# One third of a projection moved ahead of a transpose, copied twin columns and a ninth warm matmul in the first five microseconds of a fused attention and MLP kernel

## The chip, the cores and the metric

The kernel runs on one core of one Trainium2 chip. The metric is the device time of one execution in microseconds (us), lower being better. The engines are called PE (matrix multiply), ACT (activation functions and copies), DVE (vector operations), POOL and SP (which issues most DMA). A kernel is one program with a fixed instruction order on each engine; the engines wait for each other by semaphores. All runs below are of one core, mean granted clock 1.00.

## The reference

The input x is 2048 tokens by 448 features. It is normalized per token, then used twice: by linear attention with 16 heads of 28 features, and by an MLP whose hidden layer has 1792 features. The result is `x + attention * silu(mlp)`.

```python
xn  = (x - mean(x)) / sqrt(var(x) + 1e-5)            # per token
qkv = xn @ wqkv                                      # 448 -> 3 * 448, 16 heads of 28
phi = lambda t: where(t > 0, t + 1, exp(t)) + 1e-6
# attention: kv = sum_s phi(k) v ; z = sum_s phi(k) ; o = phi(q) kv / (phi(q) z + 1e-6) ; s = o @ wo
h   = relu(xn @ w1 + b1) ** 2                        # 448 -> 1792
out = x + s * silu(h @ w2 + b2)
```

All inputs are bf16. Everything starts with the normalization of x and its transposition, because the kernel's matmuls sum over the 448 features and take them on the partitions.

## The kernel before

The kernel treats the first four tiles of 128 tokens (tiles 0 to 3) by hand. For each tile, DVE takes statistics, ACT forms the reciprocal deviation, DVE writes the normalized tile `xn`, PE transposes it in chunks of 128 columns, and ACT or DVE copies the transposed chunks from PSUM to `xT`. Because 448 is three chunks of 128 and one of 64, the last 64 columns are stored twice (the "twin" columns), so that chunk 3 is a full 128 columns and its two halves can serve two matmuls of 64 rows side by side.

```python
def ln_norm(si, part=None):      # normalized columns of tile si; tiles 0 and 1 in two parts
    c = (slice(0, D if si > 3 else 384), slice(0, 256), slice(256, 384))[0 if part is None else part + 1]
    ...  # dve tensor_scalar: xn[:, si, c] = (x_tok[:, si, c] - mean) * rstd

def ln_twin(lo, hi, eng="dve"):  # tiles 4 and up: copy columns 384..448 to 448..512
    ...  # tensor_copy(xn[:, lo:hi, 448:512], xn[:, lo:hi, 384:448])

def ln_last(si):                 # tiles 0 to 3: columns 384..448 formed twice, from x itself
    ...  # dve tensor_scalar over a view of x that repeats the 64 columns; writes xn[:, si, 384:512]

def pe_transpose(si, part, eng): # part 0: chunks 0 and 1; part 1: chunks 2 and 3; None: all four
    b = Buf("T")                 # one PSUM bank
    ...  # one PE transpose per chunk
    if (si, part) == (0, 0):     # tile 0, part 0 is copied chunk by chunk
        head["xT00a"] = add(eng, lambda e, x: ev(e, x, 0, 1), [b], [("xT", 0, "a")], 0.25)
        return add(eng, lambda e, x: ev(e, x, 1, 1), [b], names, 0.25)
    return add(eng, ev, [b], names, ...)

# the PE order of the head ("turn" transposes and copies a part of a tile)
warm(8, wide=True)                                        # 8 matmuls of 512 columns on constants
turn(0, 0, "act")                                         # T00
turn(0, 1, "act")                                         # T01
turn(1, 0, "act")                                         # T10
mains(k0, (0,), [("xT", 0, "a")] + wnames("wk")[:1])      # K0, first third
mains(k0, (1,), [("xT", 0, 0)])
mains(k0, (2,), [("xT", 0, 1)])
turn(1, 1, "act")                                         # T11
mains(k1, (0, 1), [("xT", 1, 0)] + wnames("wk")[:1])      # K1, needs xT10
h_mains(0, (0, 1))                                        # first MLP tile, needs w1
...
head["xT2"] = pe_transpose(2, None, "act")                # T2
h_mains(3)
head["xT3"] = pe_transpose(3, None, "dve")                # T3
```

K0 and K1 are the key and value part of wk's product for tiles 0 and 1, each in three matmuls of 512 columns (one per chunk of 128 features). The PE order is the program order above; a matmul that waits holds up all that follow.

## Time and profile before

| | before |
|---|---|
| median of 3 runs | 141.24 us (141.20 to 141.33) |
| span of the profiled execution | 139.7 us |
| PE busy | 136.6 us, 98% |
| first matmul of K0 / of K1 | 4.92 us / 5.68 us |

The page of the kernel before: busy time with its share of the span and the number of instructions, then the chain that ended last, by engine.

```profile
PE 136.6 (98%) x1255; PEld 68.0 (49%) x1255; DVE 92.2 (66%) x226; ACT 77.8 (56%) x152; POOL 25.0 (18%) x33
...
PE 95%; DVE 2%; DMA 2%; issue 0%; DVEq 0%
```

PE is the bottleneck. What happens before PE has a continuous stream is what a change of the head can move. The timeline of the same kernel, PE only; columns are the start, the time covered, engine, line, operation, what it writes and reads, and how many instructions were merged.

```profile
2.41 1.49 PE L1062 MATMUL pb<-ones 128*128 128x512 bf16 x3
4.09 1.00 PE L528 MATMUL pb<-ident,xn 128*128 128x128 bf16 x6 [0.19 <-DVE xn L486]
4.92 0.81 PE L641 MATMUL pb<-w_qkv,xT 128*128 128x512 bf16 x3
5.57 0.28 PE L528 MATMUL pb<-ident,xn 128*128 128x128 bf16 x2
5.68 0.59 PE L641 MATMUL pb<-w_qkv,xT 128*128 128x512 bf16 x2
```

The first line is the end of the warm matmuls. Line 528 is the transposes: four of tile 0 and two of tile 1, spread out from 4.09 on. Line 641 is K0 at 4.92 (three matmuls in 0.81 us: two spacings of 0.216 and one record of 0.38), then T11, then K1 at 5.68. From 4.92 the starts follow each other without a hole.

Two more lines, from the timelines of DVE and of ACT: when tile 0's statistics start (released by the DMA of x), and when ACT copies T10.

```profile
2.22 0.63 DVE L463 BATCH_NORM_STATS2 st<-x_tok 128x6 f32<-128x448 bf16 x1 [2.02 <-DMA x_tok<-in_A_x_dram]
```

```profile
5.14 0.38 ACT L538 ACTIVATE xT<-pb 128x256 bf16<-128x256 bf16 x1
```

### The profile page before, as it was taken

What the parts mean: (1) busy time and instruction counts of PE and PEld (TensorE: products, weight loads), DVE (VectorE), ACT (ScalarE), POOL (GpSimd) and SP (SyncE); (2) the same over time, 40 slices, a digit from 0 to 9 for tenths busy, and PEclk for the clock granted to TensorE, in tenths of its full rate; (3) what the DMA queues carried; (4) which work ended last, traced back from release to release, by engine and by line L of the source; (5) the groups of instructions that cost most, each with busy time, mean ns of one, the idle gap of its engine ahead of it and who ended that gap; (6) DMA issues with size and microseconds to landing.
All of it is one profiled execution on the core that took longest, in us unless ns stands there. A gap on an engine that the chain in (4) does not pass through costs nothing.

```text
span 139.7 us, 3106 instructions
## 1 busy us (share of the span) xinstructions
PE 136.6 (98%) x1255; PEld 68.0 (49%) x1255; DVE 92.2 (66%) x226; ACT 77.8 (56%) x152; POOL 25.0 (18%) x33
## 2 busy tenths in 40 slices
PE   9999999999999999999999999999999999999992
PEld 2474444444444444444455455645555555555481
DVE  3989899799878994889995900329636071542653
ACT  4769787879988878979788912422033030301220
POOL 6000000000000000000893000000002328091770
DMA  6997367999723200000000148960000103111122
GB/s 190 247 335 219 77 170 186 356 276 144 131 52 70 60 6 0 0 19 5 0 0 0 42 120 169 175 107 0 0 0 5 66 0 101 35 66 66 38 99 68
DMA packets 20354, 12.91 MB, mean 92 GB/s; under 512 B 9524, under 2 KB 19956, under 8 KB 20340
## 3 DMA queue, kind: packets, MB, share of 16 engines
q1 hardware_dynamic: 18332, 11.52, 33.3%
q10 hardware_dynamic: 2008, 1.20, 4.3%
q8 instruction: 10, 0.16, 0.5%
q14 instruction: 4, 0.03, 0.1%
HBM read 8.78 MB, written 2.10 MB: 78 GB/s over the span
## 4 chain that ended last, share of the span: by engine, by line
PE 95%; DVE 2%; DMA 2%; issue 0%; DVEq 0%
PE pb L955 31%; PE pb L688 30%; PE pb L641 9%; PE pb L1021 8%; PE pb L722 7%; PE pb L672 6%; DMA x_tok<-in_A_x_dram 2%; PE pb L528 1%; PE pb L728 1%; DVE st L463 1%; PE pb L815 1%; PE pb L776 1%; PE pb L853 0%; DVE xn L991 0%; DVE mv L464 0%; PE pb L846 0%
## 5 line engine op out<-in xcount | busy, mean ns | idle before, releaser
L688 PE MATMUL pb<-xT,w 64*128 64x512 bf16 (+2 forms) x408 | 51.6, 365 | 0.0
L955 PE MATMUL pb<-w,r 64*128 64x448 bf16 (+3 forms) x406 | 44.9, 343 | 0.0
L697 ACT ACTIVATE r<-pb,b1f 128x512 bf16<-128x512 f32 x56 | 35.1, 688 | 4.2 <-PE pb L688 4.2
L688 PEld LDWEIGHTS pb<-xT,w 64*128 64x128 bf16 (+1 forms) x408 | 22.8, 94 | 22.5 <-ACT r L697 0.5
L955 PEld LDWEIGHTS pb<-w,r 64*128 64x128 bf16 (+1 forms) x406 | 22.8, 95 | 19.9 <-issue 0.7
L966 DVE TENSOR_TENSOR gbuf<-pb,b2b 128x448 bf16<-128x448 f32 (+1 forms) x16 | 9.2, 608 | 30.0 <-PE pb L955 30.0
L931 ACT ACTIVATE gbuf<-gbuf 128x448 bf16<-128x448 bf16 (+1 forms) x16 | 8.7, 565 | 36.0 <-DVE gbuf L966 35.5
L1000 POOL TENSOR_TENSOR xn<-xn,x_tok 128x448 bf16<-128x448 bf16 x15 | 15.0, 1032 | 46.3 <-DVE xn L991 46.3
L641 PE MATMUL pb<-w_qkv,xT 64*128 64x512 bf16 (+1 forms) x106 | 17.8, 376 | 0.0
L672 PE MATMUL pb<-xT,w_qkv 64*128 64x512 bf16 x84 | 15.5, 376 | 0.0
L705 DVE TENSOR_TENSOR r<-r 128x512 bf16<-128x512 bf16 x42 | 14.4, 418 | 0.0
L390 POOL MEMSET kvm<- 128x2048 bf16 x1 | 1.8, 1804 | 63.4 <-DVE zb L666 63.4
L1021 PE MATMUL pb<-msb,pqT 64*128 64x448 bf16 (+3 forms) x93 | 10.9, 343 | 0.0
L629 DVE SCALAR_TENSOR_TENSOR qk<-pb,qk 128x512 bf16<-128x512 f32 x16 | 10.6, 685 | 0.2
L463 DVE BATCH_NORM_STATS2 st<-x_tok 128x6 f32<-128x448 bf16 x16 | 9.3, 610 | 2.0 <-DMA x_tok<-in_A_x_dram 2.0
L991 DVE TENSOR_TENSOR xn<-pb,gbuf 128x448 bf16<-128x448 f32 (+2 forms) x17 | 9.2, 591 | 2.0 <-ACT gbuf L931 1.5
L619 ACT ACTIVATE qk<-pb 128x512 bf16<-128x512 f32 x16 | 8.9, 593 | 3.0 <-PE pb L641 2.5
L641 PEld LDWEIGHTS pb<-w_qkv,xT 64*128 64x128 bf16 (+1 forms) x106 | 6.7, 94 | 6.0 <-ACT xT L538 0.2
L722 PE MATMUL pb<-qk,xn 128*128 128x448 bf16 x48 | 9.3, 353 | 0.0
L619 ACT ACTIVATE pqT<-pb 128x512 bf16<-128x512 f32 x12 | 6.8, 597 | 3.2 <-PE pb L688 1.6
L672 PEld LDWEIGHTS pb<-xT,w_qkv 64*128 64x128 bf16 x84 | 6.0, 94 | 5.0
L706 ACT ACTIVATE r<-r 128x512 bf16<-128x512 bf16 x14 | 8.4, 637 | 0.0
(71 smaller groups left out, 99.7 us busy)
## 6 DMA issues: line engine op xcount, KB each, us to landing
out_dram<-xn SPq DMA_DIRECT2D x15, 112.0 KB, 1.7
w<-in_B_w_dram SPq DMA_DIRECT2D x1, 1568.0 KB, 10.0
x_tok<-in_A_x_dram SPq DMA_DIRECT2D x3, 448.0 KB, 3.8
xT<-rows ACTq DMA_DIRECT2D x6, 112.0 KB
w<-in_B_w_dram SPq DMA_DIRECT2D x1, 576.0 KB, 4.6
xT<-rows SPq DMA_DIRECT2D x5, 112.0 KB
w_o<-in_A_wo_dram SPq DMA_DIRECT2D x1, 392.0 KB, 11.3
w_qkv<-in_A_wqkv_dram SPq DMA_DIRECT2D x1, 384.0 KB, 3.6
```

The source lines that it names most:

```text
L463: add("dve", lambda e, _: e.bn_stats(st6[:, si, :], x_tok[:, si, :]), [("x", si)], [("st", si)], 0.58),
L619: add("act", lambda e, _: e.activation(out=slot, in_=src(), func=AF.Exp), [buf, "actw"], [tile], 0.6)
L629: lambda e, _: e.scalar_tensor_tensor(out=slot, in0=src(), scalar=1.0 + 1e-6, in1=slot, op0=ALU.add, op1=ALU.max),
L641: return e.matmul(ps(b)[:, 0:512], xT[half[h], c, si * P : (si + 1) * P], w_qkv[half[h], c, 384 : 2 * D], start=start, stop=stop,)
L672: return e.matmul(ps(b)[:, 0:512], w_qkv[half[h], c, m * P : (m + 1) * P], xT[half[h], c, g * 512 : (g + 1) * 512], start=start, stop=stop,)
L688: return e.matmul(ps(b)[:, c0 : c0 + n], w_1[half[h], c, fi * P : (fi + 1) * P], xT[half[h], c, t : t + n], start=start, stop=stop,)
L697: lambda e, _: e.activation(out=slot, in_=ps(b)[:, 0:512], func=AF.Relu, bias=b1f[:, fi : fi + 1]),
L705: return e.tensor_tensor(out=slot, in0=slot, in1=slot, op=ALU.mult)
L722: last = e.matmul(ps(b)[:, 0:D], xn[:, si, c * P : (c + 1) * P], pk_of(si), start=(si == 0), stop=(si == NT - 1),)
L955: return e.matmul(ps(b)[:, 0:n], r2[half[h], fi, si * P : (si + 1) * P], w_2[half[h], fi, c], start=start, stop=stop)
L1000: eng, lambda e, _: e.tensor_tensor(out=ob, in0=ob, in1=x_tok[:, si, c], op=ALU.add),
L1021: return e.matmul(ps(b)[:, 0:n], q, m, start=start, stop=stop)
```

## The change

There are three parts. (1) K0's first third is put ahead of T10, so that PE has a matmul to do while DVE still works on tile 1. (2) Tiles 1 to 3 get all 448 columns in one pass and copy the twins, where they had formed them from x; only tile 0 keeps the old form. (3) A ninth warm matmul fills PE's hole between the warm matmuls and T00. The scheduled order on ACT, POOL and SP is the same in both kernels; only these PE and DVE instructions differ.

```diff
-            c = (slice(0, D if si > 3 else 384), slice(0, 256), slice(256, 384))[0 if part is None else part + 1]
+            c = (slice(0, D), slice(0, 256), slice(256, D if si else 384))[0 if part is None else part + 1]
...
-            twin = head[f"xd{i}"] = ln_last(i)
+            twin = head[f"xd{i}"] = ln_twin(i, i + 1, "dve") if i else ln_last(i)
...
-        warm(8, wide=True)
+        warm(9, wide=True)
...
+        mains(k0, (0,), [("xT", 0, "a")] + wnames("wk")[:1])
         turn(1, 0, "act")
-        mains(k0, (0,), [("xT", 0, "a")] + wnames("wk")[:1])
...
-            ("dve", "st0 mv0 ... st3 mv3 xd2 xn2 xd3 xn3 xT3"),
+            ("dve", "st0 mv0 ... st3 mv3 xn2 xd2 xn3 xd3 xT3"),
```

## The prediction

> **What bounds the kernel.** TensorE. The page has PE busy 136.6 of 139.7 us, and the chain that ended last is PE for 95%. From 4.92 us the matmul records start back to back (0.216 us for 512 columns), with two small holes before 9 us: 0.10 us at 8.16 (a weight load waiting for a DMA) and 0.14 us at 8.70 (waiting for the copy xT of tile 3, which itself follows the PE). So only the first 5 us can change, and what the PE gains or loses there shifts everything after it.
>
> **The head before (timeline, records of PE, ACT, DVE).** Warm matmuls start every 0.427 us; the eighth, at 3.27, streams until 3.69. The PE then idles to 4.09, where T00 (tile 0, chunks 0 and 1) starts, released by DVE xn. Chunks 2 and 3 follow at 4.31 and 4.53, each behind its DVE producer. T10 (tile 1) follows at 4.80 and 4.87, again behind DVE xn (end 4.74). K0's first third starts at 4.92. Its input, the ACT copy xT00a, ended at 4.79, so it could have started at about 4.84.
>
> **What the change does.**
> 1. K0's first third no longer stands behind T10. It gains at most 4.92 - 4.84 = 0.08 us of start.
> 2. T10 now waits out a 0.216 us matmul: its pair runs at about 5.09 and 5.15, not 4.80 and 4.87. The ACT copy xT10 moves with it: transpose 0.22, handover 0.04, copy 0.38, handover 0.05.
> 3. The ninth warm matmul runs from 3.69 to 4.12. T00 was ready at 4.09, so T00 and xT00a come 0.03 us later, and K0's first third starts at about 4.875. The clock goes up near 4.8 (records of 0.29 us at 4.53, 0.23 at 4.80, 0.22 after). The Trainium skill, "TensorE: Matmul & The Clock Gate", Part 1, says that a busy window of about 3.4 us releases it and that the window is free-running; the hole of 0.4 us did not prevent the release here, so filling it should change little (30%: it comes earlier).
> 4. DVE: tile 1's xn11 grows from 128 to 192 columns (0.31 us, about 0.33 after), and the twin forms (0.31 us each) become copies (about 0.17, estimated from 0.20 for two tiles) that wait for their producer. st2 moves under 0.03 us; T2 and T3 get their last inputs before the PE reaches them. Worth nothing.
>
> **On the critical path.** K1's first third needs xT10. Before, that ended at 5.52 and K1 followed in PE order at 5.68. After: T10 ends at 5.37, xT10 at 5.78, K1 starts at about 5.84, though the PE reaches it at 5.75. Later work is in PE order, so the loss of 0.16 us stays; only the DMA hole at 8.16 closes, which the hole at 8.70 gives back. If the clock rises before 4.1 us instead, the loss shrinks to about 0.04.
>
> **Prediction.** 141.37 us, 8 in 10 between 141.15 and 141.55. Faster by over 2%: 0.005; within 2%: 0.99; slower by over 2%: 0.005.
>
> **What would show it.** Step 1: K0's first third at 4.84 to 4.90. Step 2: xT10 starting at 5.40 instead of 5.14, and a new PE hole of 0.09 us behind ACT xT just before K1. Step 3: T00 at 4.12, and the first 0.22 us record at the same time as before. Step 4: DVE busy down some 0.2 us.
>
> **What would make it wrong.** An earlier clock release; x landing at another time; ACT's copies overlapping more than I read, so that K1 does not wait; a window phase that differs in the timed runs by more than 0.16 us.

## The result, and the profile after

| | before | after |
|---|---|---|
| median, runs of the same rounds | 141.30 us (141.20 to 141.58, 6 runs) | 141.57 us (141.25 to 141.78, 6 runs) |
| ratio of the runs | | 1.0015, 95% interval 0.9999 to 1.0031 |
| span of the profiled execution | 139.7 us | 140.3 us |
| first matmul of K0 / of K1 | 4.92 / 5.68 us | 5.05 / 6.29 us |

A ratio is the mean time of one kernel's runs over that of the other's of the same rounds, so it is not quite the ratio of the medians. The page of the changed kernel, busy time and chain:

```profile
PE 137.3 (98%) x1256; PEld 68.5 (49%) x1256; DVE 92.1 (66%) x226; ACT 77.9 (56%) x152; POOL 25.0 (18%) x33
...
PE 98%; DVE 0%; issue 0%; DVEq 0%
```

PE is busier by 0.7 us, with one warm matmul more and some records that are longer. The Trainium skill, "Trainium Kernel Development and Optimization", Performance Expectations, warns that matmul busy time is a bad metric for how close a kernel is to roofline, because matmuls are pipelined. Busy time misleads here too, if for another reason: the useful work is the same, and reads as 0.7 us more because of the warm matmul and the cold records. The timeline of the changed kernel, PE, against the lines of before:

```profile
2.41 1.91 PE L1062 MATMUL pb<-ones 128*128 128x512 bf16 x4
4.29 0.73 PE L528 MATMUL pb<-ident,xn 128*128 128x128 bf16 x4
5.05 0.61 PE L641 MATMUL pb<-w_qkv,xT 128*128 128x512 bf16 x1
5.45 0.36 PE L528 MATMUL pb<-ident,xn 128*128 128x128 bf16 x2
5.65 0.59 PE L641 MATMUL pb<-w_qkv,xT 128*128 128x512 bf16 x2
6.08 0.27 PE L528 MATMUL pb<-ident,xn 128*128 128x128 bf16 x2
6.29 0.60 PE L641 MATMUL pb<-w_qkv,xT 128*128 128x512 bf16 x2
```

And tile 0's statistics and the ACT copy of T10 (views as before):

```profile
2.43 0.63 DVE L463 BATCH_NORM_STATS2 st<-x_tok 128x6 f32<-128x448 bf16 x1 [2.23 <-DMA x_tok<-in_A_x_dram]
```

```profile
5.85 0.38 ACT L538 ACTIVATE xT<-pb 128x256 bf16<-128x256 bf16 x1 [0.41 <-PE pb L528]
```

K1 starts 0.61 us later than before. Three things are mixed in this number:

- x landed later: statistics at 2.43 instead of 2.22, so 0.21 us. DVE's first instruction of x is ahead of everything that was changed.
- K0's first matmul took 0.61 us for its record, where the same matmul took 0.38 before, and the next start came 0.40 us after it, not 0.22. PE ran at half speed: in this execution the clock rose only near 5.6 us, in the one before near 4.8.
- The order: T10 stood behind that matmul, its copy started at 5.85, and K1 waited for it. T11's second transpose starts at 6.137 in the trace, K1 would follow 0.056 later at 6.193, and it starts at 6.289: a hole of 0.096 us.

To separate these, I use one length in every trace from here on: from the start of T00 to the start of K1's first third, called **T00 to K1**. It takes out when x lands: T00 came 1.86 us after the start of tile 0's statistics in the unchanged kernel and in the changed one. It was 1.595 before (5.681 - 4.086) and 2.001 after (6.289 - 4.288).

### The profile page after: what moved, and what is told of

It reads as the page before. It is cut to its first block, busy times and chain, and to the rows that moved or that the text cites. A ratio compares the mean times of both kernels' runs of the same rounds, so it can differ in the third digit from the quotient of the medians.

```text
span 140.3 us, 3108 instructions
## 1 busy us (share of the span) xinstructions
PE 137.3 (98%) x1256; PEld 68.5 (49%) x1256; DVE 92.1 (66%) x226; ACT 77.9 (56%) x152; POOL 25.0 (18%) x33
## 4 chain that ended last, share of the span: by engine, by line
PE 98%; DVE 0%; issue 0%; DVEq 0%
PE pb L955 30%; PE pb L688 30%; PE pb L641 9%; PE pb L1021 8%; PE pb L722 7%; PE pb L672 6%; PE pb L1062 3%; PE pb L728 1%; PE pb L528 1%; PE pb L815 1%; PE pb L776 1%; PE pb L853 0%; DVE xn L991 0%; PE pb L846 0%; DVE xn L1000 0%
## 5 line engine op out<-in xcount | busy, mean ns | idle before, releaser
L641 PE MATMUL pb<-w_qkv,xT 64*128 64x512 bf16 (+1 forms) x106 | 18.3, 379 | 0.0
```

The lines of the kernel that those rows point to most:

```text
L641: return e.matmul(ps(b)[:, 0:512], xT[half[h], c, si * P : (si + 1) * P], w_qkv[half[h], c, 384 : 2 * D], start=start, stop=stop,)
```

## The experiments

Twelve runs were made, two of them of unaltered kernels. Every run was numerically correct. All but the four delayed ones are within 0.3% of the kernel before, so the times decide little, and the traces decide.

### The parts one by one

`e1_order` (the swap alone), `e2_nine` (the ninth warm matmul alone), `e3_twins` (the twins alone), and `e4_nine_twins` (everything but the swap), against before in five rounds on one chip.

```diff
 # e1: only the swap                              # e2: only
+        mains(k0, (0,), ...)                     -        warm(8, wide=True)
         turn(1, 0, "act")                        +        warm(9, wide=True)
-        mains(k0, (0,), ...)
 # e3: only ln_norm, ln_twin and the DVE order    # e4: e2 and e3 together
```

> Only the order is changed (K0's first third ahead of T10; eight warm matmuls, old twins). Landmark: from the start of T00 to the start of K1's first third; it was 1.60 us before and 2.00 us after the whole change, which takes out when x lands. Theory A (order and clock together): the late T10 makes K1 wait for the ACT copy xT10, a hole of about 0.09 us before K1; landmark 1.72 to 1.76 if the clock rises before K0's first third, 1.95 to 2.05 if it rises after it; time 0.10 to 0.25 us over before. Rival B (the ninth warm matmul or the twins cost it): landmark about 1.60, no hole, time within 0.08 us of before. Rival C (the clock alone, which varies from run to run): no hole, the landmark goes with the time of the rise only.

> Only the ninth warm matmul is added. Theory A: T00 starts when its DVE input is there or at 4.12 us, whichever is later: at most 0.04 us, landmark 1.60 if the clock rises at about 4.8; time within 0.08 us of before. Rival B: it is the ninth matmul that moves the rise of the clock (4.81 us before, 5.60 after the change): rise near 5.6 again, time 0.2 us over before. If filling the hole helps the clock as intended, the rise comes at 4.4 or earlier.

> Only the twins of tiles 1 to 3 become copies. Theory A: DVE does as much by the time the PE asks; T2 starts in PE order with no DVE wait (the 0.01 us one before it goes), landmark 1.60, time within 0.08 us of before. Rival B: the copies that wait for their producer delay st2 or T11, time 0.1 us or more over before.

> The changed kernel with the order alone undone. Theory A: no hole before K1, time within 0.08 us of before and 0.1 to 0.25 us under the changed kernel. Rival B: as slow as the changed kernel.

| | median us (range, runs) | ratio to before (95%) | T00 to K1 |
|---|---|---|---|
| before, same rounds | 141.41 (141.21 to 143.19, 11) | 1 | |
| e1_order | 141.44 (141.31 to 141.55, 5) | 0.9991 (0.9944 to 1.0037) | 1.632 |
| e2_nine | 141.60 (141.54 to 141.84, 5) | 1.0008 (0.9966 to 1.0050) | 1.593 |
| e3_twins | 141.58 (141.19 to 141.94, 6) | 1.0000 (0.9960 to 1.0040) | 1.598 |
| e4_nine_twins | 141.45 (141.26 to 141.59, 5) | 0.9994 (0.9952 to 1.0035) | 1.979 |

No time can be told from another. (The run of 143.19 us is among those of before; without it the four ratios would be 1.0001, 1.0016, 1.0009 and 1.0002.) The lengths can, and they overthrew part of what I expected. `e4`, which has the old order, is almost as slow to K1 as the changed kernel; `e1`, which has the new order, is quick. The timeline of e4, PE:

```profile
4.20 1.11 PE L528 MATMUL pb<-ident,xn 128*128 128x128 bf16 x6
5.10 1.13 PE L641 MATMUL pb<-w_qkv,xT 128*128 128x512 bf16 x3
...
6.18 0.59 PE L641 MATMUL pb<-w_qkv,xT 128*128 128x512 bf16 x2
```

K0's three matmuls fill 1.13 us, not 0.81 as before: the first two started cold (records of 0.634 and 0.487 us). The timeline of e1, PE:

```profile
4.20 0.68 PE L528 MATMUL pb<-ident,xn 128*128 128x128 bf16 x4 [0.30 <-DVE xn L486]
4.86 0.39 PE L641 MATMUL pb<-w_qkv,xT 128*128 128x512 bf16 x1
...
5.63 0.28 PE L528 MATMUL pb<-ident,xn 128*128 128x128 bf16 x2
5.83 0.60 PE L641 MATMUL pb<-w_qkv,xT 128*128 128x512 bf16 x2
```

Here the clock was already up at T00 (records of 0.23 us, not 0.29). The swap does what it promises: K0 starts 0.66 us after T00, against 0.84 before (and 0.84 in e3, which has the old order and an early clock). But T11's second transpose is at 5.682, so K1 could have started at 5.738 and starts at 5.834, the same hole of 0.096. T00 to K1 is 1.632, against 1.595 before and 1.598 in e3, so the swap costs 0.03 to 0.04 us with an early clock. I had written 1.72 as the least in the expectation, for a clock that rises between T00 and K0; I had forgotten there the still earlier clock for which the prediction itself had said 0.04. And the expected 0.10 to 0.25 us in the time of e1 did not show either.

The trace of `e2` gives the ninth matmul nothing to answer for (its times are another matter, see below): T00 to K1 is 1.593, the clock rises near 4.65 us, neither at 4.4 or earlier, as the intent would have it, nor near 5.6, as the rival would. It showed one thing by chance. In that execution the x of tiles 2 and 3 landed late, at 5.37 us instead of 4.73, and T3 waited 0.15 us for DVE. The timeline of e2, DVE's last step for tile 3, PE's weight load and the first transposes of T3:

```profile
7.79 0.37 DVE L486 TENSOR_SCALAR xn<-x_tok,mv,rstd 128x384 bf16<-128x384 bf16 x1
...
8.22 0.23 PEld L528 LDWEIGHTS pb<-ident,xn 128*128 128x128 bf16 x4 [0.27 <-DVE xn L486]
```

With the old twins, xn of tile 3 is the last thing DVE makes; in the kernel before it ended at 7.87, and PE asked for it at 7.94. `e3` makes it ahead of its twin: there it ended 3.585 us after T00, against 3.779 before, and T3 followed in PE order at 3.835. So the twins' part makes tile 3 robust against a late x, by 0.19 us, and no more: in e3 itself nothing waited for it. The DVE timeline of before, tiles 2 and 3 (twin, norm, twin, norm), and of the changed kernel (norm, copy, norm, copy):

```profile
6.71 0.31 DVE L512 TENSOR_SCALAR xn<-x_tok,mv,rstd 128x128 bf16<-128x128 bf16 x1
6.94 0.37 DVE L486 TENSOR_SCALAR xn<-x_tok,mv,rstd 128x384 bf16<-128x384 bf16 x1
7.26 0.31 DVE L512 TENSOR_SCALAR xn<-x_tok,mv,rstd 128x128 bf16<-128x128 bf16 x1
7.49 0.37 DVE L486 TENSOR_SCALAR xn<-x_tok,mv,rstd 128x384 bf16<-128x384 bf16 x1
```

```profile
7.23 0.40 DVE L486 TENSOR_SCALAR xn<-x_tok,mv,rstd 128x448 bf16<-128x448 bf16 x1 [0.36 <-ACT rstd L477]
7.66 0.18 DVE L501 COPY xn<-xn 128x64 bf16<-128x64 bf16 x1
7.75 0.39 DVE L486 TENSOR_SCALAR xn<-x_tok,mv,rstd 128x448 bf16<-128x448 bf16 x1
8.18 0.18 DVE L501 COPY xn<-xn 128x64 bf16<-128x64 bf16 x1
```

The copies are shorter (0.18 for 0.31), but each waits for its producer's end, and the old forms overlapped: in both, the four instructions take 1.13 to 1.15 us from first start to last end.

### The clock taken out

If the rise of the clock is what blurs the picture, then a kernel whose head starts after the rise must show the swap alone. Ten dummy statistics on DVE (on the constant row, to a scratch tile) hold tile 0 back by about 4 us, and 14 more warm matmuls, gated on them, keep PE at work. By then x and the weights of the head have landed too. These kernels are slower on purpose.

```diff
+        for i in range(10):
+            head[f"dl{i}"] = add("dve", lambda e, _, i=i: e.bn_stats(dly[:, i, :], junk), ["ones"], [("dly", i)], 0.6)
...
-        warm(8, wide=True)          # (9 in the changed kernel)
+        warm(8, wide=True)
+        warm(6, wide=True, after=[("dly", 5)])
+        warm(8, wide=True, after=[("dly", 9)])
...
-            ("dve", "st0 mv0 ...
+            ("dve", "dl0 ... dl9 st0 mv0 ...
```

`e5_late_old` is the kernel before with this delay, `e6_late_new` the changed kernel (with 8 first warm matmuls, so without the ninth), `e7_late_twins` the twins alone. `e8_late_two` takes the old twins and puts two thirds of K0 ahead of T10 (`turn(1, 0, "act")` behind `mains(k0, (1,), ...)`), a larger dose of the same medicine.

> The kernel before, with ten dummy statistics on DVE ahead of tile 0 (about 6 us) and more warm matmuls behind them, so that in every execution the clock is up and x and weights have landed when T00 starts. A reference for the three below, not an attempt to be fast: about 145.5 us. Theory A (the spread between runs and between kernels is the moment the clock rises and x lands): the five runs lie within 0.15 us of each other, where before spread over 0.3 us and more; landmark T00 to K1 1.59 to 1.61. Rival C (the spread comes from elsewhere): as wide as before.

> The whole change under the same delay and the same warm matmuls. Theory A: with the clock up, the order costs only the wait for xT10, about 0.04 us: landmark 1.63, K1 behind a hole of about 0.09 us, time 0.00 to 0.06 us over the late old kernel. Rival B (the change costs 0.2 us whatever the clock does): 0.15 to 0.25 us over it. If the change pays as intended: under it.

> The twins' change alone under the same delay. Theory A: xn of tile 3 comes 0.15 to 0.2 us earlier, and nothing asks for it: time within 0.05 us of the late old kernel, landmark 1.60.

> Two thirds of K0 ahead of T10 instead of one, old twins, same delay. Theory A: T10 comes 0.22 us later still, so K1 starts at 1.83 to 1.86 behind a hole of about 0.3 us, and the time is 0.22 to 0.28 us over the late old kernel. Rival (the order does not matter, the PE does the same work in any order): landmark 1.60 to 1.65, no more than 0.05 us over it.

In all four, every transpose was recorded with at most 0.23 us, so the clock was up. The timeline of the late old kernel (T00 at 8.08, then K0 and K1), of the late new kernel (T00 and K1), and of the late kernel with two thirds ahead, PE:

```profile
8.08 0.94 PE L529 MATMUL pb<-ident,xn 128*128 128x128 bf16 x6
8.86 0.81 PE L642 MATMUL pb<-w_qkv,xT 128*128 128x512 bf16 x3
...
9.62 0.59 PE L642 MATMUL pb<-w_qkv,xT 128*128 128x512 bf16 x2
```

```profile
8.09 0.62 PE L529 MATMUL pb<-ident,xn 128*128 128x128 bf16 x4
...
9.71 0.60 PE L642 MATMUL pb<-w_qkv,xT 128*128 128x512 bf16 x2
```

```profile
8.73 0.61 PE L642 MATMUL pb<-w_qkv,xT 128*128 128x512 bf16 x2
...
9.50 0.28 PE L529 MATMUL pb<-ident,xn 128*128 128x128 bf16 x2
9.92 0.61 PE L642 MATMUL pb<-w_qkv,xT 128*128 128x512 bf16 x2
```

In the last, T11 ends its stream near 9.61 and K1 starts at 9.92, when the copy of T10 is there: a hole of 0.31 us, as expected.

| | T00 to K1 | all runs, us |
|---|---|---|
| e5_late_old | 1.540 | 145.09, 145.12, 145.19, 145.22; 146.03, 146.46 |
| e7_late_twins | 1.535 | 145.09, 145.09, 145.11, 145.14, 145.27; 146.10 |
| e6_late_new | 1.619 | 145.22, 145.27; 146.01, 146.18, 146.19, 146.29 |
| e8_late_two | 1.835 | 145.44, 145.62; 146.42, 146.42, 146.62, 146.69 |

The order matters, and in the direction of the theory: one third ahead of T10 costs 0.079 us (0.084 against e7, which has the same twins; twice the 0.04 I expected), two thirds cost 0.295, the twins nothing. Part of this is the delay's own doing: T00 came 1.90 us after tile 0's statistics here, not 1.86, because the last of the added warm matmuls held it (in e5 that matmul started at 7.865 and T00 at 8.083). In the new order K1 hangs on T00, in the old one on DVE's columns of tile 1, so a held T00 makes the swap look dearer. That is a reading, not tested. Counted from the statistics, which are not held, e6 is 0.082 behind e7. The runs fall into two groups some 0.9 us apart, which I had not expected; my forecast that the runs of e5 would lie within 0.15 us holds for the lower group only. In the lower group, the means are 145.16 (old), 145.25 (new) and 145.53 (two thirds): the differences of 0.09 and 0.37 are near those of the lengths. With two runs each for the new order and two thirds, and the upper group set aside after the fact, they are a hint and no proof.

What sets the groups apart was seen in one trace. The profiled execution of e6 was of the upper group, and its PE has one hole that the late old kernel lacks, near 43 us. The timelines of e6, PE and SP's queue:

```profile
42.03 0.59 PE L642 MATMUL pb<-w_qkv,xT 64*128 64x512 bf16 x4
43.38 0.59 PE L689 MATMUL pb<-xT,w 64*128 64x512 bf16 x3 [0.76 <-ACT r L698]
```

```profile
39.53 1.27 SPq L550 DMA_TRANSPOSE xT<-xn  x1
40.84 3.22 SPq L652 DMA_TRANSPOSE pqR<-qk  x2
```

SP took 3.22 us for the two issues after that of tile 11 (2.51 in e5), the first of them alone 1.94 instead of 1.23. The trace's semaphore record has tile 11's transposition landing at 43.29 us, against 41.93 in e5, and the weight load that needs it goes 0.06 us after the landing. The view names ACT as the releaser; ACT had been done (its last update before was at 43.01), and the DMA came last. From start to start PE lost 0.92 us there, which with the 0.08 of the head makes nearly all of the 1.00 us that e6 is behind e5 from T00 to the last matmul. Why tile 11's transposition landed late stays open: SP's slow issue was of the one behind it, so it may be a consequence as well as a sign of the same cause. The upper group held 8 of the 12 runs of e6 and e8, and 3 of the 12 of e5 and e7. Whether a later K1 makes it likelier is not tested; so I can't say that it has nothing to do with the order.

### The same kernels again, the missing combination, and a candidate

`e9_after_again` and `e10_before_again` are the two kernels unaltered. `e12_order_twins` is the changed kernel with eight warm matmuls. `e11_split` is e12 with chunk 0 of tile 0 transposed into a PSUM bank of its own, so that ACT's first copy need not wait for chunk 1. (A draft with both chunks in one bank, ordered for chunk 0 alone, was a race, since PE would write the bank that ACT reads.)

```diff
             b = Buf("T")
+            b0 = Buf("T0") if (si, part) == (0, 0) else b     # chunk 0's bank
...
-                head["xT00a"] = add(eng, lambda e, x: ev(e, x, 0, 1), [b], [("xT", 0, "a")], 0.25)
+                head["xT00a"] = add(eng, lambda e, x: ev(e, x, 0, 1), [b0], [("xT", 0, "a")], 0.25)
```

> The changed kernel once more, unaltered, for another sample of when the clock rises. Theory A (the rise falls anywhere between 3 and 6 us, and only it separates a landmark of 1.63 from one of 2.00): T00 to K1 1.63 if the clock is up before T00, 1.74 to 1.78 if it rises within 0.8 us of T00, 1.95 to 2.05 if later. Rival B (nine warm matmuls and the new order make it rise late): rise near 5.6 and landmark near 2.00 again. Time 141.3 to 141.8.

> The kernel before once more, unaltered. Theory A: landmark 1.60 if the clock is up within 0.8 us of T00, up to 1.98 if it rises later; time 141.2 to 141.8, and its runs overlap those of the changed kernel. Rival B: landmark 1.60 and 0.15 us or more under the changed kernel in each run.

> The changed kernel with eight warm matmuls. Theory A: as the changed kernel at the same moment of the rise (1.63, 1.74 to 1.78, 1.95 to 2.05), with a hole before K1 in each case. If the ninth matmul matters: another landmark at the same rise.

> The new order and twins with eight warm matmuls, and chunk 0 of tile 0 transposed into a bank of its own, so that ACT copies it without waiting for chunk 1. Theory A: K0's first third then starts about 0.08 us earlier, T10 and K1 with it: landmark 1.53 to 1.58 with an early clock (1.63 without the split), 0.05 us under the kernel before at best, which the times will not tell from it. Rival (K0's start is not what T10 waits for): 1.63.

The timeline of the unchanged kernel, second sample, PE:

```profile
4.14 1.11 PE L528 MATMUL pb<-ident,xn 128*128 128x128 bf16 x6 [0.24 <-DVE xn L486]
5.05 1.17 PE L641 MATMUL pb<-w_qkv,xT 128*128 128x512 bf16 x3
...
6.17 0.59 PE L641 MATMUL pb<-w_qkv,xT 128*128 128x512 bf16 x2
```

The timeline of the changed kernel, second sample, PE:

```profile
4.21 0.67 PE L528 MATMUL pb<-ident,xn 128*128 128x128 bf16 x4
4.87 0.39 PE L641 MATMUL pb<-w_qkv,xT 128*128 128x512 bf16 x1
...
5.84 0.60 PE L641 MATMUL pb<-w_qkv,xT 128*128 128x512 bf16 x2
```

The roles are exchanged. This time the unchanged kernel was the slow one to K1 (2.024, above the 1.98 that I had given as the most) and the changed kernel the quick one (1.631), and what differs within each pair of equal kernels is the clock. So neither the ninth matmul nor the order makes the clock late every time; rival B as I wrote it falls. That they change how often it is late is not excluded by two traces of a kernel.

The cleanest pair for the order with an early clock is e3 and e12: both have the copied twins and eight warm matmuls, both had the clock up before T00, and they differ in the order alone. The timelines of e3 and of e12, PE, T00 and K1:

```profile
4.23 1.00 PE L528 MATMUL pb<-ident,xn 128*128 128x128 bf16 x6 [0.60 <-DVE xn L486]
...
5.83 0.59 PE L641 MATMUL pb<-w_qkv,xT 128*128 128x512 bf16 x2
```

```profile
4.15 0.68 PE L528 MATMUL pb<-ident,xn 128*128 128x128 bf16 x4 [0.36 <-DVE xn L486]
...
5.78 0.61 PE L641 MATMUL pb<-w_qkv,xT 128*128 128x512 bf16 x2
```

Now all ten undelayed traces, sorted by order and clock. The second column is the start of the first PE record that is shorter than a cold one; the last is the length from T00 to the start of the last matmul of the whole kernel.

| trace | first short record, us | T00 to K1 | T00 to the last matmul |
|---|---|---|---|
| e3_twins, old order | 2.84 | 1.598 | 132.693 |
| e2_nine, old order | 4.65 | 1.593 | 132.888 (T3 waited 0.15 for DVE) |
| before, old order | 4.80 | 1.595 | 132.708 |
| e10_before_again, old order | 5.47 | 2.024 | 133.138 |
| e4_nine_twins, old order | 5.53 | 1.979 | 133.073 |
| e12_order_twins, new order | 3.27 | 1.631 | 132.853 (PE waited 0.11 for w1) |
| e9_after_again, new order | 3.69 | 1.631 | 132.734 |
| e1_order, new order | 4.20 | 1.632 | 132.905 (PE waited 0.16 at 96.7 us) |
| after, new order | 5.56 | 2.001 | 133.104 |
| e11_split, new order | 4.16 | 1.576 | 132.680 |

Whatever K1 loses, the last matmul loses too, apart from the three waits that are noted. e10 lost 0.429 to K1 against before and 0.430 at the end; after lost 0.406 and 0.396. From K1 to the last matmul every trace takes 131.09 to 131.14 us, once the three waits are taken out. That is what a saturated PE means.

The times of this batch: e9 141.66 us (141.22 to 141.91, 6 runs), ratio to before 1.0004 (0.9962 to 1.0045); e10 141.25 (141.19 to 141.60), ratio 0.9979 (0.9935 to 1.0023); e12 141.42 (141.18 to 143.05), 1.0003; e11 141.54 (141.12 to 141.76), 0.9993. Note the second: the kernel before, measured against itself in the same rounds, came out 0.21% faster, more than the 0.15% of the first result. But most of it comes from one run of 143.24 us among those of before: without it e10 is 0.06% faster, and e9, the changed kernel, 0.15% slower, as in the first result.

The times hold a hint that I had not looked for. Of the runs of the unchanged kernel, 22 of 45 are at or under 141.35 us; of the changed kernel, 2 of 12; of the other altered ones without a delay, 6 of 23 with eight warm matmuls and 1 of 10 with nine. Of the four traces with nine, two had a late clock, of the six with eight, one. The limit of 141.35 was chosen after the fact, the kernels ran on several chips, and the time of a run does not tell when its clock rose, so this may be chance. But the rival that the change, perhaps its ninth matmul, makes a late rise more frequent stands, and no run here tests it.

The split does what the theory says: K0 starts 0.60 us after T00 instead of 0.65 (0.08 was expected), K1 at 1.576 instead of 1.631. It is the first version with the new order that is ahead of the old one to K1 (1.595), by 0.02 us, and its profiled execution, 141.12 us, is the shortest of all runs. But its median is no better than the others', so it isn't shown to beat the kernel before. In e12, the MLP's first matmul waited for w1, which landed at 6.29 us. In the other nine undelayed traces it landed between 5.40 and 6.20, so this is another draw of a landing and not the faster head: e11's K1 was earlier still (5.73) and did not wait.

## Why the prediction was right or wrong

The direction (slower by a trifle) is what the lengths show; the times only lean that way, as the interval includes 1. The median of the changed kernel's six runs, 141.57, is 0.02 us over the top of my range; the ratio times the median of before, 141.30 x 1.0015 = 141.51, is inside. The size is not confirmed: the times can't resolve it. In the profiled pair the changed kernel lost 0.41 us from T00 to K1, and most of that was luck, the clock of that one execution: the pair e9 and e10 came out the other way round.

**Step 1, K0 starts earlier: right.** Seen from T00, K0 started at 0.764 instead of 0.835 with the clock still cold (after), and at 0.655 instead of 0.839 with the clock up (e1 and e9 against e3). Predicted was 4.875 - 4.12 = 0.755.

**Step 2, T10 and K1 late: the mechanism was right, the size depends on the clock.** The hole before K1 was predicted at 0.09 and measured at 0.096 in after. What it costs in T00 to K1 is 0.033 with the clock up before T00 (1.631 in e12 against 1.598 in e3, which differ in the order alone; the prediction's other case said 0.04), and 0.08 in the late kernels (e6 against e5 and e7), where T00 was held. The 0.16 of the main case, a clock that rises between T00 and K0, was never met with the new order in a trace, so it stays open. With a late clock, old and new order gave 1.98 to 2.02 and 2.00, but their clocks did not rise at quite the same moment, so no cost is read from them.

**Step 3, the clock "at the same time as before": wrong, and this is the step that failed.** I took the rise at 4.8 us for a property of the kernel, from one trace and three runs that happened to agree. The first short record started anywhere from 2.84 to 5.56 us in ten traces, in both kernels. The change alone does not decide it: the changed kernel had it at 5.56 and at 3.69, the one before at 4.80 and at 5.47. What shifts it from run to run stays open. The Trainium skill, "TensorE: Matmul & The Clock Gate", Part 1, had told me that the window is free-running; I cited it, and named an earlier release and another window phase among what could make me wrong, but did not draw the conclusion, that the head's cost is a distribution, and that one trace is one draw from it. A late rise costs 0.38 to 0.43 us (e4 and e10 against before), several times what the change does. The ninth matmul did not hold T00 up, which the prediction had put at 0.03 us: it ended its stream at 4.12, but x landed so that T00 started at 4.14 or later in each of the other nine undelayed traces; only in the trace that I predicted from (T00 at 4.09) would it have been in the way.

**Step 4, DVE worth nothing: right for the time, incomplete.** DVE busy went down by 0.17 us (92.22 to 92.05; 0.2 predicted). I had not seen that the swap of twin and norm also gives tile 3's transposes 0.19 us of slack, which matters when x lands late, as it did in e2.

**A hole misread.** I put the 0.10 us hole at 8.16 down to a DMA. The semaphore record has that DMA landing at 6.71 in the kernel before, long ahead. The hole has the same 0.096 us after the change, although PE comes there 0.60 us later, so it does not close with a later PE; similar holes (0.096 and 0.093 us) stand near 94 and 130 us, where PE also changes between matmuls of 64 rows and of more. That the change of shape is the cause is a reading, not tested.

**What went where.** The gain that was hoped for, K0 earlier, is real, 0.07 to 0.18 us of start. It is not kept, because the next thing that PE needs is not K0's result but T10's: the transposes that K0 overtook are the head of the longer chain (transpose, copy, K1). Pooling all runs of unaltered code from all batches, the kernel before has a median of 141.37 (45 runs) and the changed kernel 141.61 (12 runs), which leans the same way as the lengths but by more than the order's 0.03 to 0.08 us, and stems from different rounds and chips; chance or more frequent late rises could make up the rest, and the record can't tell which; single medians of five or six runs of kernels with the old order are as high (e2 141.60, e3 141.58).

## What to carry to other kernels

Before you move work into a hole on the bottleneck engine, ask what that engine's next waits are chained to: filling a hole with work that overtakes the head of a longer chain (here transpose, copy, next matmul) turns a hole into a later, equal one. When a change is worth a tenth of a per cent, compare lengths between two landmarks in several traces, not times, and sort the traces by what varies from run to run (here the moment the clock rises and the moment the first DMA lands). Take an unchanged kernel against itself in the same rounds: here it came out 0.21% apart, and looking at the single runs showed that one outlier made most of it.

## What the Trainium skill lacked or had wrong

- "TensorE: Matmul & The Clock Gate", Part 1, gives the transition with a spread of 500 ns either way around 4 us of sustained activity. Here, with the first matmul at 0.30 to 0.31 us in each of ten traces, the first short record started between 2.84 and 5.56 us. The spread of 2.72 us fits into the free-running window of 3.4 us which the same part states, and not into the 500 ns either way. In e3 the short record ended at 3.41 us, 3.11 after the first matmul began, so less than one whole window of matmuls was enough there.
- The same page, Part 4, says that the full clock does not engage for transposes and gives about 275 ns for one. Here a transpose was recorded with 0.29 us before the rise and 0.22 us after it, 0.056 us from start to start.
- No page says that the profile's mean granted clock can miss a late rise: it reads 1.00 in all ten undelayed traces, those with the late rise included. The record of a 512-column matmul (0.63 us before the rise, 0.38 after) tells it.
- No page mentions that the issue of a DMA transposition by SP varies: 1.23 us in e5 and 1.94 in e6 for the same instruction. The transposition ahead of it took 2.50 us from the start of its issue to landing in e5 and 3.75 in e6, where PE was held up 0.92 us.
